# Early parts of chunks 14 to 23 in slots 7 to 10, a solver that fetches ahead, and seven block products from the fifth group on

## The chip, the cores and the metric

One core of a Trainium2 chip runs the kernel. The metric is the device time of one execution in microseconds. The engines are TensorE (PE in the rows, PEld for its weight loads), VectorE (DVE), ScalarE (ACT), GpSimd (POOL) and SyncE (SP), which here only issues transfers. Each engine works through its own instructions in the order in which the program gives them, and each queue of transfers is issued in that order too.

## What is computed

The first half is a recurrence over 768 tokens for 4 batches of 8 heads with 40 values each; the second half is a feed-forward layer on its output.

```python
for t in range(S):
    y[:, :, t] = einsum('bhd,bhde->bhe', r_t, state)
    Sa = einsum('bhde,bhe->bhd', state, a_t)
    state = state * w_t[:, :, None, :] - einsum('bhd,bhe->bhde', Sa, b_t)
    state = state + einsum('bhd,bhe->bhde', v_t, k_t)
x = y.transpose(0, 2, 1, 3).reshape(3072, 320)
h = maximum(x @ w_in, 0)            # w_in 320 x 2048
out = (h * h) @ w_out               # w_out 2048 x 320
```

Everything is float32.

## The kernel before

**Chunks.** The sequence is cut into chunks of 128 tokens of one batch: 24 chunks, numbered 0 to 23, four batches by six. For each chunk there are three kinds of work.

- The *early part* (`early`, L360) needs w, a and b only. It turns w (four transposes into one PSUM bank of the pool `ps_w`, which has four), runs the first scans over it on VectorE (L372, L373), then the second scans (L377 to L381), turns b and a, multiplies them by the decays (L387, L388), and makes the products N (matmuls into `ps_w`, copies on ScalarE). It yields after each of these, so a caller takes it in six steps. The decays are built in a ring of two tiles, `decay` (L186), stored to DRAM as `kept_e`, and come back later into `dec` (`kept_here`, also two). So chunks m and m + 2 write the same decay tile, and the second must wait until the first is stored. N goes to DRAM in pieces (`kept_q`, `kept_m`, `kept_n`, and from chunk 14 on `kept_d`). `prepare` (L907) wraps it: before the first step it starts the loads of w, b and a of the next chunk (`load_early`), on SP's queue.
- The *solve* inverts the triangular matrices of several chunks at once, a *unit*, on POOL: `take` fetches `kept_d` into `half_n`, `solving` runs 63 steps (two instructions each, L478 and L480; 31 steps for the units of chunks 0 to 13), and the result goes to `kept_t`. Units 0 to 7 hold chunks 0 to 13, unit 8 holds 14 to 17, unit 9 holds 18 to 21, unit 10 holds 22 and 23. `inverses` (L500) later fetches a chunk's share as T.
- The *chain* (`chain`, L632) uses T, N, the decays and the state of the batch, in eight steps, one of which needs the one before; its last instructions on VectorE are tokens (L697) and the new state (L701).

**The feed-forward layer** (`Ffn`, L724) works on groups of two chunks. `thirds` and `whole` make h, `square` squares it on VectorE, and `make_quarter` makes the output, four quarters for each chunk. From group SEVEN on `make_piece` takes the place of `make_quarter`'s matmuls: the output of two chunks is made from seven products of 128x160 blocks in place of eight, from sums and differences of blocks of h and of the weights. The sums of the weights (`sum_weights`, L875) are kept in the two `decay` tiles (P7, P6) and the four `in_ab` tiles (P4), one changes `w_out` in place, and one output tile lies in the first `in_w` tile. These tiles are free once no early part is left.

**The order** is written by hand; the engines get it as the program emits it. A list of words (L1013) orders chunks 0 to 6 and all of the early parts up to chunk 13, with their stores. Two words near its end matter below: `sE13@g` puts the store of chunk 13's decays on POOL's own queue, and `S6.99` has POOL finish unit 6; `S7.99` follows. After the list come 17 *slots* (L1125), i = 7 to 23. In slot i, `sorted_slot` (L1064) emits chunk i's chain, the preparations of chunk i + 1 (turning r and v, the products RV, decaying the state by f, L570, turning k, turning the decays, L582, scaling k and b, the products A), up to two early parts, and four quarters of the feed-forward layer. `ahead` (L1033) says which early parts a slot takes: 14 and 15 in slot 7, 16 and 17 in slot 8, and then one a slot, 18 to 23 in slots 9 to 14. The first of them is taken at fixed points of the slot from its start on, the second from the step of `turn_state` on, near its end. `step` emits a few things and then counts down stores that were put off (`tick`, `store`). At the slot's end `loads` starts the transfers of the chunk after the next: dec, k and b.

After a slot, every unit whose chunks all have their early parts is taken and solved whole: unit 8 after slot 8, unit 9 after slot 12, unit 10 after slot 14. One buffer `half_n` holds what a unit is solved from, so a unit's fetch starts when the one before is finished.

PSUM has eight banks: four in `ps_w`, two in `ps_c`, two in `ps_f`. A new tile of a pool takes a bank whose last reader is done, and the matmul that writes it waits for that reader.

## Time and profile before

| | |
|---|---|
| median of three runs | 945.2 us (944.94 to 946.49) |
| the profiled execution | 944.9 us, of it a span of 943.2 us |
| mean granted TensorE clock | 0.956 |
| transfers | 103.41 MB, of 253269 packets 234154 are under 512 B |

Times in rows are microseconds from the span's start. A row of a timeline has the start, the duration, the engine, the line, the operation, the tile written and the tiles read, and how many instructions are merged; in brackets stands how long the engine was idle before and what ended it. A row of a window has its bounds and length, then busy time and instructions of PE, PEld, DVE, ACT and POOL, the granted clock, the DMA share and GB/s. The DMA share counts packets in flight and can exceed 1 in short windows. A row of grouped instructions has the count, the busy time, the mean duration in ns and the idle time before. tokens (L697) of chunks 7 to 11 are written at 359.40, 396.29, 432.74, 466.72 and 500.69 us, so a slot takes some 34 to 37 us there.

### The profile page before, as it was taken

How to read it: one execution, taken by the hardware profiler on the slowest of the kernel's cores; microseconds unless marked ns; L12 is line 12 of the kernel's file. 1: busy time of each engine (PE TensorE's matmuls, PEld its weight loads, DVE VectorE, ACT ScalarE, POOL GpSimd, SP SyncE). 2: the span in 40 equal slices, each digit the busy share in tenths (PEclk: the TensorE clock that was granted, in tenths of full speed). 3: DMA queues.
4: the chain of work that ended last, by engine and by line, in shares of the span. 5: the costliest groups of instructions: out<-in, count | busy, mean ns of one | idle time of the engine just before them, and what ended most of it. 6: DMA issues, size and time to landing. Idle time of an engine off the chain costs nothing.

```text
span 943.2 us, 23218 instructions
## 1 busy us (share of the span) xinstructions
PE 883.6 (94%) x9404; PEld 738.8 (78%) x9404; DVE 518.8 (55%) x1209; ACT 283.0 (30%) x735; POOL 525.1 (56%) x935
## 2 busy tenths in 40 slices
PE   6678989889999999999999999999989999999997
PEld 5466657667787887888888888888978999988897
DVE  5827657888853454553755454675634645343243
ACT  3033334544523333333333332222212222222110
POOL 4557347065007786418999959999958986000000
PEclk9858988799899999999999999999998999999999
DMA  9769779766866578987665776604355445040000
GB/s 110 127 145 143 171 136 180 184 160 129 178 101 154 93 128 161 170 163 131 126 92 87 127 178 113 115 17 86 57 131 93 74 81 99 18 75 1 22 15 15
DMA packets 253269, 103.41 MB, mean 110 GB/s; under 512 B 234154, under 2 KB 240298, under 8 KB 252010
## 3 DMA queue, kind: packets, MB, share of 16 engines
q1 hardware_dynamic: 244709, 83.00, 49.7%
q0 software_dynamic: 3760, 17.10, 7.4%
q10 hardware_dynamic: 4693, 1.83, 0.9%
q8 instruction: 74, 1.21, 0.6%
q14 instruction: 33, 0.27, 0.1%
HBM read 69.00 MB, written 30.92 MB: 106 GB/s over the span
## 4 chain that ended last, share of the span: by engine, by line
PE 47%; POOL 25%; DVE 11%; DMA 8%; issue 4%; ACT 3%; SPq 2%; ACTq 0%; DVEq 0%; POOLq 0%
PE ps_f L87 21%; POOL half_t L480 13%; POOL half_p L478 12%; PE ps_w L87 11%; PE ps_c L87 8%; PE ps_w L331 3%; DMA half_n<-kept_d 2%; PE ps_f L264 2%; DMA in_r<-in_r_dram 1%; DMA T<-kept_t 1%; SPq L513 1%; DVE half_t L480 1%; DVE half_t L478 1%; DVE decay L381 1%; DMA dec<-kept_e 1%
## 5 line engine op out<-in xcount | busy, mean ns | idle before, releaser
L478 POOL TENSOR_TENSOR half_p<-half_n,half_t 128x462 f32<-128x462 f32 (+39 forms) x406 | 229.2, 565 | 75.7 <-DMA half_n<-kept_q 23.7
L480 POOL TENSOR_TENSOR half_t<-half_t,half_p 128x462 f32<-128x462 f32 (+39 forms) x406 | 245.7, 605 | 31.8
L87 PE MATMUL ps_f<-w_out,hid 128*128 128x320 f32 (+1 forms) x768 | 165.4, 368 | 0.0
L87 PE MATMUL ps_f<-tokens,w_in 128*128 128x256 f32 x672 | 157.0, 387 | 0.0
L87 PEld LDWEIGHTS ps_f<-w_out,hid 128*128 128x128 f32 x768 | 123.2, 190 | 26.0
L87 PEld LDWEIGHTS ps_f<-tokens,w_in 128*128 128x128 f32 x672 | 125.9, 192 | 19.1 <-issue 2.0
L769 DVE TENSOR_TENSOR hid<-hid 128x512 f32<-128x512 f32 x96 | 82.3, 899 | 10.3 <-ACT hid L762 9.9
L762 ACT ACTIVATE hid<-ps_f 128x512 f32<-128x512 f32 x84 | 49.8, 596 | 80.9 <-PE ps_f L87 80.8
L372 DVE TENSOR_TENSOR_SCAN decay<-ps_w,ones 128x64 f32<-128x64 f32 x88 | 23.9, 271 | 66.1 <-PE ps_w L331 66.0
L451 POOL DMA_DIRECT2D half_n<-kept_q x18 | 9.5, 534 | 88.7 <-DMA kept_m<-N 26.4
L697 DVE TENSOR_TENSOR tokens<-ps_c,dec 128x512 f32<-128x512 f32 x24 | 16.6, 691 | 72.9 <-PE ps_c L87 71.1
L347 DVE TENSOR_TENSOR RX<-ps_w,upper 128x512 f32<-128x512 f32 x48 | 30.8, 684 | 38.4 <-PE ps_w L87 38.2
L87 PEld LDWEIGHTS ps_c<-xr,T 64*64 64x64 f32 x768 | 29.7, 146 | 25.2 <-issue 18.4
L264 PE MATMUL ps_f<-ident 128*128 128x512 f32 (+3 forms) x108 | 49.4, 591 | 0.0
L87 PE MATMUL ps_f<-tokens,w_third 64*128 64x256 f32 x336 | 47.6, 394 | 0.1
L398 ACT COPY N<-ps_w 128x256 f32<-128x256 f32 x48 | 17.7, 369 | 94.9 <-PE ps_w L87 67.7
L548 DVE TENSOR_TENSOR kvT<-ps_w,dec 128x512 f32<-128x512 f32 x24 | 16.4, 684 | 52.5 <-PE ps_w L331 23.3
L87 PE MATMUL ps_c<-xr,T 64*64 64x40 f32 x768 | 35.7, 240 | 10.1 <-DMA T<-kept_t 5.4
L347 DVE TENSOR_TENSOR RV<-ps_w,upper 128x512 f32<-128x512 f32 x48 | 30.9, 685 | 21.2 <-PE ps_w L87 20.9
L658 ACT COPY minus_x<-ps_c 64x160 f32<-64x160 f32 x96 | 27.5, 287 | 36.5 <-PE ps_c L87 32.6
L331 PE MATMUL ps_w<-ident,in_ab 128*128 128x128 f32 x184 | 28.5, 301 | 10.1 <-DVE RV L347 8.1
L87 PE MATMUL ps_w<-rT,kvT 40*128 40x128 f32 x384 | 31.4, 308 | 5.4 <-ACT kvT L561 5.1
(167 smaller groups left out, 1548.9 us busy)
## 6 DMA issues: line engine op xcount, KB each, us to landing
dec<-kept_e SPq DMA_DIRECT2D x22, 633.8 KB
kept_e<-decay SPq DMA_DIRECT2D x19, 633.8 KB
in_w<-in_w_dram SPq DMA_DIRECT2D x24, 160.0 KB
in_b<-in_b_dram SPq DMA_DIRECT2D x24, 160.0 KB
in_ab<-in_a_dram SPq DMA_DIRECT2D x24, 160.0 KB
in_r<-in_r_dram SPq DMA_DIRECT2D x24, 160.0 KB
in_v<-in_v_dram SPq DMA_DIRECT2D x24, 160.0 KB
in_k<-in_k_dram SPq DMA_DIRECT2D x22, 160.0 KB
```

Source lines behind the costliest of these rows:

```text
L87: nc.tensor.matmul(o, l_, r_, start=start, stop=True, skip_group_check=True)
L264: nc.tensor.matmul(fill_bank[:, :n * 128], ident, ident.unsqueeze(1).to_broadcast([128, n, 128]), start=True, stop=True, skip_group_check= ...
L331: nc.tensor.transpose(p_[:, q * 128:(q + 1) * 128], pair(x_, q), ident)
L347: nc.vector.tensor_tensor(t_, p_, over4(upper), Alu.mult)
L372: nc.vector.tensor_tensor_scan(up[:, q, MID + 1:C + 1], wT[:, q, MID:], ones, 1.0, Alu.mult, Alu.mult)
L398: nc.scalar.copy(plain, p_[:, ::2].rearrange("s h (f t) -> s f h t", f=2))
L478: eng.tensor_tensor(p_, part[:, at:at + m_].unsqueeze(1).to_broadcast([128, n, m_]), t3[:, :n, s:s + 1].to_broadcast([128, n, m_]), Alu.mult)
L480: eng.tensor_tensor(t3[:, :n, s + 1:], t3[:, :n, s + 1:], p_, Alu.subtract)
L658: nc.scalar.copy(flipped(xn)[halves[half], flip, :, :, :D], by_pair(xs[halves[half ^ flip]]))
L697: nc.vector.tensor_tensor(t_, y_, g["up"][:, :, :C], Alu.mult)
L762: nc.scalar.activation(h_, p_.rearrange("p f t -> p (f t)"), Act.Relu)
L769: nc.vector.tensor_tensor(h_, h_, h_, Alu.mult)
```

## The change

- `ahead` puts the early parts of chunks 14, 15 and 16 into slot 7, of 17, 18 and 19 into slot 8, of 20 and 21 into slot 9, of 22 and 23 into slot 10. Slots 11 to 14 have none.
- A slot has 14 numbered places (`at_place`), most of them at the end of a step. The first early part of a slot takes its six steps at places 1 to 6, a middle one (made[1] of three) at 5 to 10, the last one at 9 to 14. Place 1 follows the turning of r and v, place 3 f and the decay of the state, place 4 the products RV and `thirds`, place 6 `whole`, place 8 precedes the turn of k, place 9 follows the turn of the decays, place 10 precedes the transposes of the chain's result, place 11 follows the scaling of k and b, place 12 the products A, place 13 `whole`, place 14 stands at the slot's end.
- Units are solved by `solve_more`: the first 32 rows' words of the next unit are fetched while the last 23 steps of the one before run, and unit 8 starts at place 9 of slot 8, unit 9 at the end of slot 9, unit 10 at the end of slot 10 (in POOL's order, each behind the unit before).
- SEVEN is 4 and not 6: groups 4 and 5 (chunks 8 to 11) take seven products too. The sums of the weights move from slots 15 and 16 to slots 11 and 12, the first of them to a point ahead of f, the second to a point behind f rather than behind the turn of k; the other two keep their points within a slot.
- In the last group the two last products get PSUM banks of their own, the additions of the two products before are done ahead of the last product, and chunk 23's output tile is stored one piece earlier.

```diff
+            last = g == len(order) // GB - 1
-            if at in (0, 3, 4):
-                self.bank = psum(ps_f)
+            fresh = at in ((0, 3, 4, 5, 6) if last else (0, 3, 4))
+            if fresh:
+                self.bank = psum(ps_w if at > 4 else ps_f)
...
+            if at == 4:
+                self.sixth = ps[0]
+            if at == (4 if last else 6):
+                plus(hi1, self.sixth, hi1)
+                plus(hi0, self.sixth, hi0)
+                less(lo1, hi1, lo1)
+            if at == 5:
+                self.fifth = ps[1]
+            if at == (5 if last else 6):
+                plus(hi1, self.fifth, hi1)
+                plus(hi0, self.fifth, hi0)
             if at == 6:
                 plus(hi0, ps[2], hi0)
-                plus(hi1, ps[0], hi1)
-                plus(hi0, ps[0], hi0)
-                less(lo1, hi1, lo1)
-                plus(hi0, ps[1], hi0)
-                plus(hi1, ps[1], hi1)
-                for n, o_ in enumerate(self.ends):
-                    bb, c = order[g * GB + n]
-                    row = bb * S + c * C
-                    store(out[row:row + C, :], o_, 2)
+            for n in {5: (1,), 6: (0,)}.get(at, ()) if last else (1, 0) if at == 6 else ():
+                bb, c = order[g * GB + n]
+                row = bb * S + c * C
+                store(out[row:row + C, :], self.ends[n], 2)
...
-    SEVEN = 6
+    SEVEN = 4
...
-    ahead = {7: (14, 15), 8: (16, 17)}
-    ahead.update({i: (i + 9,) for i in range(9, len(order) - 9)})
+    ahead = {7: (14, 15, 16), 8: (17, 18, 19), 9: (20, 21), 10: (22, 23)}
...
-    unit = len(solves)
+    under_way = [len(solves), None]
+
+    def solve_more():
+
+        u, now = under_way
+        while u < len(units) and all(m_ in done for m_ in range(len(order)) if unit_of[m_] == u):
+            flush()
+            take(u, own, slice(0, EARLIER))
+            if now is not None:
+                run(now)
+            take(u, own, slice(EARLIER, None))
+            now = solving(u, (40,))
+            next(now)
+            u += 1
+        if u == len(units) and now is not None:
+            run(now)
+            now = None
+        under_way[:] = u, now
...
-        one, two = (made + [iter(()), iter(())])[:2]
+        parts = [(gen, 1) for gen in made[:1]] + [(gen, 5) for gen in made[1:-1]] + [(gen, 9) for gen in made[1:][-1:]]
+        place = [0]
+
+        def at_place():
+            place[0] += 1
+            for gen, first in parts:
+                if first <= place[0] < first + 6:
+                    next(gen, None)
+            if i == 8 and place[0] == 9:
+                done.add(ahead[i][0])
+                solve_more()
...
-        step(of(turn_rv), on(one), on(one))
+        step(of(turn_rv), at_place)
         fetch_next(j + 1, "r")
-        step(second.make_quarter)
-        step(on(ch), of(decay_state))
-        if i == 2 * SEVEN + 3:
-            sum_weights(0)
-        if i == 2 * SEVEN + 4:
-            sum_weights(3)
-        step(of(make_rv), second.thirds)
-        step(on(ch), on(one))
+        sums(0)
+        step(second.make_quarter, at_place)
+        step(on(ch), of(decay_state), at_place)
+        sums(1, 3)
+        step(of(make_rv), second.thirds, at_place)
+        step(on(ch), at_place)
         if fine:
             join()
-        step(second.whole)
-        step(on(ch))
-        step(on(one), of(turn_k))
+        step(second.whole, at_place)
+        step(on(ch), at_place)
+        step(at_place, of(turn_k))
-        step(of(turn_down))
-        step(on(one), on(ch))
-        step(on(ch), of(scale_kb))
+        step(of(turn_down), at_place)
+        step(at_place, on(ch))
+        step(on(ch), of(scale_kb), at_place)
...
-        step(second.square, second.make_quarter, on(two), on(two))
-        if i in ahead and len(ahead[i]) > 1:
-            step(on(two), on(two))
-        step(second.make_quarter, on(two))
+        step(second.square, second.make_quarter, at_place)
+        step(second.make_quarter)
...
-        done.update(ahead.get(i, ()))
         sorted_slot(i, g, ch)
-        while unit < len(units) and all(m_ in done for m_ in range(len(order)) if unit_of[m_] == unit):
-            flush()
-            take(unit, own)
-            solve(unit)
-            unit += 1
+        done.update(ahead.get(i, ()))
+        solve_more()
```

More of the change, by code (lines that the diff above doesn't have):

```diff
@@ L797, in make_piece @@
         def make_piece(self, g, at):
-            names = "P1 P4 P2 P7 P6 P5 P3" if g == len(order) // GB - 1 else "P4 P1 P2 P7 P6 P5 P3"
+            last = g == len(order) // GB - 1
+            names = "P1 P4 P2 P7 P6 P5 P3" if last else "P4 P1 P2 P7 P6 P5 P3"
             if at == 7:
@@ L820, in make_piece @@
                 k, e, m_ = n // 4, n // 2 % 2, n % 2
-                mm(ps[part], x_[:, n], seven[name][k * QF + 2 * m_ + e], at in (0, 3, 4) and n == 0)
+                mm(ps[part], x_[:, n], seven[name][k * QF + 2 * m_ + e], fresh and n == 0)
             self.quarter += 1
@@ L1076, in sorted_slot, with sums @@
         of = lambda fn: (lambda: fn(j, n)) if more else (lambda: None)
+        def sums(*which_):
+            for n_ in which_:
+                if i == 2 * SEVEN + 3 + n_ // 3:
+                    sum_weights(n_)
         if more and "x" in n:
@@ L1084, in sorted_slot @@
             join()
-        step(of(turn_rv), on(one), on(one))
+        step(of(turn_rv), at_place)
         fetch_next(j + 1, "r")
-        step(second.make_quarter)
-        step(on(ch), of(decay_state))
-        if i == 2 * SEVEN + 3:
-            sum_weights(0)
-        if i == 2 * SEVEN + 4:
-            sum_weights(3)
-        step(of(make_rv), second.thirds)
-        step(on(ch), on(one))
+        sums(0)
[4 more added lines that the diff above has]
+        step(on(ch), at_place)
         if fine:
             join()
-        step(second.whole)
-        step(on(ch))
-        step(on(one), of(turn_k))
-        if i == 2 * SEVEN + 3:
-            sum_weights(1)
-        step(of(turn_down))
-        step(on(one), on(ch))
-        step(on(ch), of(scale_kb))
+        step(second.whole, at_place)
[4 more added lines that the diff above has]
+        step(on(ch), of(scale_kb), at_place)
         if fine:
             join()
-        step(on(ch), of(make_a), second.thirds, on(one))
+        step(on(ch), of(make_a), second.thirds, at_place)
         fetch_next(j + 1, "v")
-        step(of(turn_state), second.square, second.whole, on(two))
-        if i == 2 * SEVEN + 3:
-            sum_weights(2)
+        step(of(turn_state), second.square, second.whole, at_place)
+        sums(2)
         if not early_join and not fine:
@@ L1117, in sorted_slot @@
         loads(j + 1)
-        step(second.square, second.make_quarter, on(two), on(two))
-        if i in ahead and len(ahead[i]) > 1:
-            step(on(two), on(two))
-        step(second.make_quarter, on(two))
-        for gen in (one, two, joining):
+        step(second.square, second.make_quarter, at_place)
+        step(second.make_quarter)
+        for gen in made + [joining]:
             run(gen)
```

2 lines of the change are left out of this document (1 added, 1 removed).

## The prediction, on record before the changed kernel ran

> **What bounds the kernel now.** I read the busy shares first, then the windows by slot, the waits of TensorE, and the timeline of each engine and of the SP queue around slots 7 to 10, where the early parts go.
>
> ```profile
> PE 883.6 (94%) x9404; PEld 738.8 (78%) x9404; DVE 518.8 (55%) x1209; ACT 283.0 (30%) x735; POOL 525.1 (56%) x935
> 396.30:432.70 36.40, 35.96 (x444) 30.20 (x440) 20.23 (x60) 13.52 (x39) 8.22 (x17) 1.00 0.99 168
> PE ps_c L87 <- DMA T<-kept_t: 5.4, 1, 5.4
> ```
>
> TensorE is busy for 94% of the span, and from slot 7 on it hardly stops (35.96 of 36.40 us in the window about slot 8). So a microsecond that TensorE waits there is lost, and work that only changes its slot is free. After 330 us its one long wait is for T of chunk 18, the inverse that POOL solves as part of unit 9. The same window has a DMA share of 0.99 with two early parts in a slot; the change asks for three in slots 7 and 8.
>
> **What the change gains.** The wait for T, and what follows it:
>
> ```profile
> 479.64 0.66 PE L87 MATMUL ps_c<-xr,T 64*64 64x40 f32 x16
> ...
> 482.19 0.66 PE L87 MATMUL ps_c<-minus_x,N 64*64 64x40 f32 x16
> ...
> 708.54 1.08 PE L87 MATMUL ps_c<-xr,T 64*64 64x40 f32 x16 [5.36 <-DMA T<-kept_t]
> ...
> 713.27 0.66 PE L87 MATMUL ps_c<-minus_x,N 64*64 64x40 f32 x16
> ```
>
> ```profile
> 706.00:708.00 2.00, 0.00 (x0) 0.00 (x0) 0.00 (x0) 0.00 (x0) 0.15 (x1) 0.62 0.92 170
> 708.00:710.00 2.00, 1.46 (x20) 1.41 (x22) 0.00 (x0) 0.32 (x2) 1.61 (x6) 0.50 0.05 13
> ```
>
> ```profile
> 415.18 1.04 POOL L451 DMA_DIRECT2D half_n<-kept_d  x2 [25.14 <-DMA kept_d<-N]
> 693.76 0.60 POOL L487 DMA_DIRECT2D kept_t<-half_t  x1 [0.30 <-POOL half_t L480]
> ```
>
> The wait is 5.36 us. Behind it the clock is at half, and the stretch from the product with T to the one with N takes 713.27 - 708.54 = 4.73 us, against 482.19 - 479.64 = 2.55 us for the same work in slot 11. Together 5.36 + 2.18 = 7.5 us. POOL works from 415.18 to 693.76 on units 8 and 9. In the new order chunk 17 is ready by place 6 of slot 8, so unit 8 starts some 10 us earlier even if that slot is late, and the first words of unit 9 come in beneath unit 8's last steps. T of unit 9 then lands tens of us before its use if TensorE is late itself, and 10 to 20 us before it if not. I count the whole **-7.5**.
>
> The clock's price is told by the Trainium skill too (TensorE: Matmul & The Clock Gate, Part 1): an idle window of about 3.4 us halves the clock, and about 3.4 us of work restores it. By that an interruption would cost some 1.7 us behind it, not the 2.2 measured here. The trace decides.
>
> Two more groups take seven products:
>
> ```profile
> L87 PE MATMUL ps_f<-w_out,hid 128*128 128x320 f32 x32 | 9.0, 436 | 0.0
> ...
> L87 PE MATMUL ps_f<-w_out,hid 128*128 128x160 f32 x32 | 4.5, 299 | 0.0
> L87 PE MATMUL ps_f<-in_ab,hid 128*128 128x160 f32 x16 | 2.7, 312 | 0.1
> L87 PE MATMUL ps_f<-decay,hid 128*128 128x160 f32 x16 | 2.3, 299 | 0.0
> ...
> L87 PE MATMUL ps_f<-w_out,hid 128*128 128x160 f32 x32 | 4.5, 299 | 0.0
> L87 PE MATMUL ps_f<-decay,hid 128*128 128x160 f32 x16 | 2.4, 306 | 0.0
> ```
>
> The first row is one slot with the plain product (568.3 to 601.1 us), the next three and the last two are slots with block products (from 662.8 and 759.8). A group is two slots: 18.0 us plain, 9.5 + 6.9 = 16.4 us in blocks, so 1.6 us less; the busy sums count overlapping edges twice, more of them in blocks, so I take 2.0. Two groups: **-4.0** (3.2 to 5). Its additions on VectorE lie beside matmuls, in slots that lose an early part, and the weight sums move with it at the same cost.
>
> The tail of the last group:
>
> ```profile
> 938.44 0.33 DVE L825 TENSOR_TENSOR o<-ps_f,o 128x160 f32<-128x160 f32 x1 [6.19 <-PE ps_f L87]
> ...
> 939.61 0.32 DVE L825 TENSOR_TENSOR in_w<-ps_f,in_w 128x160 f32<-128x160 f32 x1
> ...
> 940.11 0.42 SPq L110 DMA_DIRECT2D out_dram<-in_w  x1
> ```
>
> One of the six additions stays behind the last matmul, and one store, issued at about 938.8 in place of 940.11: **-1.3**. The small wait for bT when a second early part is run in one go at a slot's end (below, 0.44) goes too: **-0.4**. Gains: 7.5 + 4.0 + 1.3 + 0.4 = 13.2 us.
>
> **What it costs.** An early part moved from slots 11 to 14 into slots 7 to 10 carries these matmuls, and nine transfers on SP's queue:
>
> ```profile
> 476.95 0.60 PE L331 MATMUL ps_w<-ident,in_w 128*128 128x128 f32 x4
> ...
> 487.02 1.09 PE L331 MATMUL ps_w<-ident,in_ab 128*128 128x128 f32 x8
> ...
> 493.64 1.06 PE L87 MATMUL ps_w<-decay,bT 40*128 40x128 f32 x16
> ```
>
> That is 0.60 + 1.09 + 1.06 = 2.75, with overlaps some 2.4 us, paid now or later. The price is in the order. Slot 7, now:
>
> ```profile
> 334.37 0.60 PE L331 MATMUL ps_w<-ident,in_w 128*128 128x128 f32 x4
> ...
> 339.61 0.66 PE L87 MATMUL ps_c<-minus_x,N 64*64 64x40 f32 x16
> ...
> 344.44 1.09 PE L331 MATMUL ps_w<-ident,in_ab 128*128 128x128 f32 x8
> ...
> 346.61 0.66 PE L582 MATMUL ps_w<-ident,dec 128*128 128x128 f32 x4 [0.63 <-DVE decay L381]
> ...
> 367.27 1.16 PE L87 MATMUL ps_w<-decay,bT 40*128 40x128 f32 x16 [0.44 <-DVE decay L388]
> ```
>
> ```profile
> 341.88 0.17 DVE L570 TENSOR_TENSOR f<-end,dec 128x4 f32<-128x4 f32 x1 [5.32 <-DMA dec<-kept_e]
> ...
> 344.32 0.17 DVE L377 RECIPROCAL decay<-decay 128x4 f32<-128x4 f32 x1
> ...
> 361.99 0.29 DVE L372 TENSOR_TENSOR_SCAN decay<-ps_w,ones 128x64 f32<-128x64 f32 x1
> ...
> 363.28 0.27 DVE L373 TENSOR_TENSOR_SCAN decay<-ps_w,ones 128x64 f32<-128x64 f32 x1
> ```
>
> *First, the second decay tile.* The ring `decay` has two tiles, so chunk 15 writes the tile of chunk 13, and must wait until chunk 13's decays have been stored. Chunk 15 now writes at 361.99. The store goes out on POOL, behind the steps of a solve:
>
> ```profile
> 353.82 0.56 POOL L390 DMA_DIRECT2D kept_e<-decay  x1
> ```
>
> ```profile
> kept_e<-decay POOLq DMA_DIRECT2D x1, 633.8 KB, 5.8
> ```
>
> So the tile is free at 353.82 + 5.8 = 359.6. In the new order chunk 15 is made[1]: turned at place 5, scanned at place 6, which VectorE reaches near 348. VectorE works in order, so the first scans stand until 359.6; behind them wait the other scans, kvT, the scaling of k and b, the masks RX and A. First scans 363.28 + 0.27 - 361.99 = 1.5 us, second scans 346.61 - 344.32 = 2.3 us: done at 363.4. TensorE goes on with chunk 14's product, chunk 15's turns and k, until it runs out of PSUM: of the four ps_w banks one holds chunk 15's turned w until the second scans have read it, and the other three wait for VectorE's products behind them. So the turn of the decays (L582) cannot begin before 363.4; now it begins at 346.61. That is 16.8 us later, of which 2.4 are work done earlier: 14.4, and about 1.4 more for the clock, since part of the slow stretch waits for bT anyway. **+15.8** (12 if the store lands sooner or the clock holds, 18).
>
> An earlier wait in slot 7 lies inside this one: chunk 14's b and a are now turned at place 4, at about 340 and not 344.44, and the fourth bank is that of its w, whose second scans now stand behind f (341.88, held up by the decays of chunk 8) rather than behind RV. That is 5 us of waiting, but the point at 363.4 does not move with it.
>
> *Second, slot 8's loads.* Chunk 18 is fetched when chunk 17 starts (place 1) and turned at place 5, four places later; now a second part starts only near the slot's end. SP's queue in slots 7 and 8:
>
> ```profile
> 360.06 1.20 SPq L146 DMA_DIRECT2D in_w<-in_w_dram  x1
> ...
> 362.91 6.41 SPq L710 DMA_DIRECT2D tokens<-tokens  x8
> 369.43 0.47 SPq L1049 DMA_DIRECT2D dec<-kept_e  x1
> ...
> 378.11 4.63 SPq L110 DMA_DIRECT2D kept_d<-N  x4
> ...
> 383.40 0.58 SPq L146 DMA_DIRECT2D in_w<-in_w_dram  x1
> ```
>
> The fetch asked for at slot 8's start goes out at 383.40, because the decays, k, b, blocks, N and the stores stand before it. One fetch of three leaves the place ahead of the tokens (362.91 - 360.06 = 2.9 us) and one store of decays (0.5), so about 380 on this slot's clock, and in_w lands perhaps 4 us later (between 2 and the 5.8 of the larger store): 384. Place 5 comes at about 378. TensorE waits 0 to 6 us, with the clock 0 to 8.5; I take **+5**, below the middle of what the queue gives, because slot 7's stop lets the queue drain.
>
> *Third, the last part of a slot* is scanned at places 10 and 11, between kvT and RX; its four microseconds of scans stand before the masks and hold a bank that the products A need. By the same scans (1.5 + 2.3 us) against some 3 us of TensorE work: about 1.2 us in each of slots 8, 9 and 10, with one wait for bT: **+3** (0 to 5).
>
> *Fourth, slot 10*, whose f waits for its decays as well:
>
> ```profile
> 447.35 0.17 DVE L570 TENSOR_TENSOR f<-end,dec 128x4 f32<-128x4 f32 x1 [2.18 <-DMA dec<-kept_e]
> ```
>
> As in slot 7 the turns of place 4 now stand behind it: **+1** (0 to 2.5).
>
> Sum: 15.8 + 5 + 3 + 1 - 13.2 = +11.6 on the profiled execution's 944.9 us, which lies 0.3 below the median of 945.2: 956.5; I say **956.5 us**. Its own range, with all bounds of one sign, is 946 to 967.
>
> **The rivals.** *A, the tile is free in time.* If the store of chunk 13 landed by about 348, or the scans of chunk 15 reached VectorE only at 360, the 15.8 and its sequel vanish, as the slot then runs as the two-part slots do now: 944.9 - 13.2 = 931.7, at worst 935 with the smaller waits. From a landing near 350 on, it is no longer faster: 13.2 of gains less 9 of other costs leaves 4. For it: POOL would run quicker while VectorE stands. Against: the store is behind POOL's steps, and nothing before slot 7 is changed. Chance 0.10.
>
> *B, the stop in slot 7 alone.* The queue drains during it, so that slots 8 to 10 cost nothing: 944.9 - 13.2 + 15.8 = 947.5, or 943 to 945 where the block products give the upper end. For it: SP idles while TensorE stands. Against: the fetch's place in the queue. Chance 0.12.
>
> *C, the queue does not recover.* With three stores and three fetches a slot against a DMA share of 0.99 every transfer of slots 8 to 10 comes late, the decays first, and each slot has a stop like slot 7's first, 5 + 2 us: 956.5 + 14 = 970. Against: with one part a slot, that share fell back by itself. Chance 0.05.
>
> **How the numbers follow.** Forecast 0.73, A 0.10, B 0.12, C 0.05. 943 to 968 holds nearly all of the forecast and most of B, 0.8 together. A measurement of this kernel tells 0.2%, 1.9 us, from no change. Faster: A, and a little of B and the forecast's low end, 0.14. Same (943.3 to 947.1): half of B, 0.07. Slower: the rest, 0.79.
>
> **What would show it.** Right: in slot 7 VectorE's first scans of the second early part waiting some 11 us for kept_e, TensorE's turn of dec waiting for decay L381, slot 7 about 18 us longer, the granted clock at half behind it; a wait of TensorE for in_w in slot 8; no wait for T near 700; fewer than six additions behind the last matmul. Wrong: slots 7 and 8 of some 39 us each, or a second early part whose scans find their tile free.

## The result, and the profile after

The changed kernel takes 975.25 us (median of 5 runs, 972.57 to 979.39), the kernel before 944.94 us beside it (942.95 to 946.49). The ratio is **1.0322 [1.0289, 1.0355]**: 30 us slower, where 11.6 were forecast and 968 was the upper end of the range. The profiled execution took 973.1 us with a span of 971.4.

The windows of the changed kernel from one chunk's tokens to the next, for chunks 7, 8, 11 and 12 (columns as in the table of windows shown for the kernel before: length, busy time of PE, PEld, DVE, ACT and POOL, granted clock, DMA share, GB/s):

```profile
322.30:381.20 58.90, 46.22 (x450) 38.03 (x450) 26.97 (x82) 16.87 (x49) 44.34 (x114) 0.83 0.65 128
381.20:431.40 50.20, 43.78 (x481) 35.69 (x477) 25.06 (x81) 16.03 (x47) 13.44 (x34) 0.90 0.77 158
...
511.80:546.80 35.00, 33.46 (x411) 26.99 (x405) 20.11 (x26) 11.61 (x31) 32.49 (x33) 1.00 0.52 101
546.80:581.50 34.70, 32.15 (x394) 26.08 (x390) 12.58 (x21) 9.41 (x23) 24.50 (x46) 1.00 0.46 103
```

The first two of them in the kernel before:

```profile
323.30:359.40 36.10, 35.47 (x416) 29.66 (x416) 16.62 (x43) 14.59 (x41) 26.74 (x69) 1.00 0.64 123
359.40:396.30 36.90, 36.46 (x451) 30.76 (x447) 20.50 (x61) 13.65 (x39) 23.42 (x63) 1.00 0.82 153
```

I call such a stretch a row, by the chunk whose tokens end it (VectorE's L697). The first row was 36.13 us before, the second 36.89. Both now lose time twice: TensorE stands for 12.7 and 6.4 us of them, and their mean granted clock is 0.83 and 0.90 where it was 1.00. All rows, from the same instruction in both traces, beside what the prediction's terms add up to (its 2.4 us of moved work per part counted in rows 7 to 10 and taken off from row 11 on):

| rows | before | after | difference | forecast |
|---|---|---|---|---|
| start to tokens of chunk 6 | 323.27 | 322.27 | -1.0 | 0 |
| 7 | 36.13 | 58.98 | +22.9 | +17.8 |
| 8 | 36.89 | 50.14 | +13.3 | +8.4 |
| 9 | 36.45 | 39.47 | +3.0 | +3.4 |
| 10 | 33.98 | 40.92 | +6.9 | +4.4 |
| 11 and 12 | 67.94 | 69.74 | +1.8 | -4.8 |
| 13 to 17 | 158.88 | 149.00 | -9.9 | -8.8 |
| 18 | 35.82 | 28.49 | -7.3 | -7.5 |
| 19 to 23 | 142.93 | 142.93 | 0.0 | 0 |
| tokens of chunk 23 to the end | 70.9 | 69.5 | -1.4 | -1.3 |

The gains came as forecast, 18.6 us against 17.6 in the last rows with the moved work. The costs were 18.7 us higher than forecast: 5.1 in row 7, 4.9 in row 8, 2.5 in row 10 and 6.6 in rows 11 and 12, less 0.4 in row 9.

What TensorE waited for after 322 us (sum, times, longest):

```profile
PE ps_w L331 <- issue: 9.5, 2, 7.7
PE ps_c L671 <- ACT minus_x L658: 5.8, 5, 2.5
PE ps_w L331 <- DVE decay L381: 4.9, 1, 4.9
PE ps_w L331 <- DMA in_w<-in_w_dram: 3.9, 1, 3.9
PE ps_w L87 <- ACT xnT L673: 1.6, 1, 1.6
```

The wait for T is gone. In its place are these five kinds of wait in rows 7 to 12 (of the rest, none sums to over 0.8 us). Row 7, from the timelines of TensorE and VectorE, and windows of 4 us:

```profile
344.14 1.09 PE L331 MATMUL ps_w<-ident,in_ab 128*128 128x128 f32 x4 [4.88 <-DVE decay L381]
...
358.28 0.29 DVE L372 TENSOR_TENSOR_SCAN decay<-ps_w,ones 128x64 f32<-128x64 f32 x1 [11.56 <-DMA kept_e<-decay]
...
362.21 1.09 PE L331 MATMUL ps_w<-ident,in_ab 128*128 128x128 f32 x4 [7.72 <-issue]
...
363.94 1.06 PE L582 MATMUL ps_w<-ident,dec 128*128 128x128 f32 x4
```

```profile
344.00:348.00 4.00, 3.86 (x27) 3.29 (x28) 2.72 (x5) 1.38 (x4) 3.29 (x10) 0.50 1.31 178
...
356.00:360.00 4.00, 0.00 (x0) 0.00 (x0) 1.69 (x10) 0.25 (x1) 0.07 (x1) 0.62 0.98 261
360.00:364.00 4.00, 1.79 (x9) 1.82 (x10) 2.11 (x10) 0.00 (x0) 3.14 (x12) 0.50 0.42 71
364.00:368.00 4.00, 3.92 (x25) 3.11 (x23) 3.73 (x12) 0.00 (x0) 3.29 (x10) 0.50 0.49 100
368.00:372.00 4.00, 4.00 (x56) 3.63 (x54) 2.65 (x12) 3.09 (x11) 3.37 (x9) 0.67 0.47 129
```

This is the stop that the prediction described: VectorE stands 11.56 us for the store of chunk 13, and the turn of dec starts at 363.94, where the prediction has 363.4 as its earliest time. In part that nearness is chance, as the row itself starts 1.0 us sooner here (322.27 against 323.27): from the row's start it is 41.67 us, and 40.1 by the prediction. Behind the stop the clock stays at half to about 370.

Row 8, from the timelines of SP's queue, TensorE and ScalarE:

```profile
399.86 0.59 SPq L146 DMA_DIRECT2D in_w<-in_w_dram  x1
...
403.64 1.09 PE L331 MATMUL ps_w<-ident,in_w 128*128 128x128 f32 x4 [3.95 <-DMA in_w<-in_w_dram]
...
417.16 0.37 ACT L398 COPY N<-ps_w 128x256 f32<-128x256 f32 x1 [3.13 <-DMA kept_n<-N]
...
419.98 1.16 PE L87 MATMUL ps_w<-rT,xnT 40*128 40x128 f32 x16 [1.57 <-ACT xnT L673]
```

The late w is there. Not foreseen is the second half: the one tile N of an early part is still being stored when the next part wants it, ScalarE waits with its copies, and the copy to xnT, which the chain needs, stands behind them in ScalarE's order.

The gains, from the timelines of TensorE and VectorE: chunk 18's products without a wait, and one addition behind the last matmul.

```profile
740.09 0.66 PE L87 MATMUL ps_c<-xr,T 64*64 64x40 f32 x16
...
742.91 0.66 PE L87 MATMUL ps_c<-minus_x,N 64*64 64x40 f32 x16
...
968.09 0.33 DVE L827 TENSOR_TENSOR o<-ps_w,o 128x160 f32<-128x160 f32 x1 [1.62 <-PE ps_w L87]
```

### The profile page after: what moved, and what is told of

Read it like the earlier page. It is cut to its first block, busy times and chain, and to the rows that moved or that the text cites. A ratio compares the mean times of both kernels' runs of the same rounds, so it can differ in the third digit from the quotient of the medians.

```text
span 971.4 us, 23479 instructions
## 1 busy us (share of the span) xinstructions
PE 893.6 (92%) x9500; PEld 750.5 (77%) x9500; DVE 531.9 (55%) x1233; ACT 283.1 (29%) x735; POOL 531.7 (55%) x943
## 4 chain that ended last, share of the span: by engine, by line
PE 75%; DVE 8%; DMA 6%; ACT 5%; issue 4%; SPq 2%; POOL 0%; ACTq 0%; DVEq 0%; POOLq 0%
PE ps_f L87 37%; PE ps_w L87 15%; PE ps_c L87 12%; PE ps_w L331 5%; PE ps_f L264 2%; PE ps_c L671 1%; DMA blocks<-kept_t 1%; ACT N L401 1%; PE ps_c L598 1%; DMA hid<-in_moe_w_in_dram 1%; SPq L420 1%; DVE half_t L478 1%; DVE half_t L480 1%; PE ps_w L582 1%; DMA dec<-kept_e 1%
## 5 line engine op out<-in xcount | busy, mean ns | idle before, releaser
L480 POOL TENSOR_TENSOR half_t<-half_t,half_p 128x462 f32<-128x462 f32 (+39 forms) x406 | 250.5, 617 | 31.8
L87 PE MATMUL ps_f<-tokens,w_in 128*128 128x256 f32 x672 | 160.5, 394 | 0.0
L87 PEld LDWEIGHTS ps_f<-tokens,w_in 128*128 128x128 f32 x672 | 128.8, 197 | 20.1 <-issue 2.2
L87 PE MATMUL ps_f<-w_out,hid 128*128 128x160 f32 (+1 forms) x736 | 143.4, 348 | 0.0
L87 PEld LDWEIGHTS ps_f<-w_out,hid 128*128 128x128 f32 x736 | 112.7, 190 | 17.3
L769 DVE TENSOR_TENSOR hid<-hid 128x512 f32<-128x512 f32 x96 | 78.8, 862 | 9.9 <-ACT hid L762 9.4
L331 PE MATMUL ps_w<-ident,in_ab 128*128 128x128 f32 x184 | 30.6, 310 | 25.9 <-issue 10.6
L697 DVE TENSOR_TENSOR tokens<-ps_c,dec 128x512 f32<-128x512 f32 x24 | 16.6, 691 | 64.6 <-PE ps_c L87 62.8
L331 PEld LDWEIGHTS ps_w<-ident,in_ab 128*128 128x128 f32 x184 | 23.2, 158 | 32.5 <-issue 17.6
L87 PE MATMUL ps_f<-decay,hid 128*128 128x160 f32 x256 | 38.0, 302 | 0.4 <-DVE hid L828 0.4
```

The costliest lines, as they stand in the source:

```text
L87: nc.tensor.matmul(o, l_, r_, start=start, stop=True, skip_group_check=True)
L331: nc.tensor.transpose(p_[:, q * 128:(q + 1) * 128], pair(x_, q), ident)
L480: eng.tensor_tensor(t3[:, :n, s + 1:], t3[:, :n, s + 1:], p_, Alu.subtract)
L697: nc.vector.tensor_tensor(t_, y_, g["up"][:, :, :C], Alu.mult)
L769: nc.vector.tensor_tensor(h_, h_, h_, Alu.mult)
```

## The experiments

Ratios are to the kernel before, run beside each. The start to chunk 6's tokens took between 316.8 and 323.3 us in the profiles though hardly anything differs there, so I compare rows first and totals second.

**The store of chunk 13 alone.**

```diff
-... D8 sE13@g K7 S7.99 lk8
+... D8 sE13 K7 S7.99 lk8
```

> One edit to the changed kernel (973.1 us profiled, 975.25 median): the store of chunk 13's decays goes out on SP's queue and not on POOL's, behind the steps of a solve. Theory of the prediction (chunk 15's scans wait for that store): VectorE's wait of 11.56 us for kept_e at L372 and TensorE's second stop in slot 7 (7.72 us at the turn of b and a) go; slot 7 (r-turn to tokens, 48.75 us) falls to about 35, since the first stop (4.88 us at place 4, and its clock) stays; total 958 to 966. Rival (three early parts are simply too much for slot 7, whatever the tile): another wait takes its place, slot 7 stays over 44 us and the total over 970.

Measured: 967.76 us, ratio 1.0260 [1.0233, 1.0288]. Row 7 is 53.29 us and not 58.98: 5.7 less, where about 14 was expected. Timelines of VectorE and TensorE in this kernel, and its windows:

```profile
347.41 0.29 DVE L372 TENSOR_TENSOR_SCAN decay<-ps_w,ones 128x64 f32<-128x64 f32 x1 [0.60 <-PE ps_w L331]
...
362.91 2.08 PE L87 MATMUL ps_w<-rT,xnT 40*128 40x128 f32 x16 [2.87 <-ACT xnT L673]
```

```profile
360.00:364.00 4.00, 1.14 (x14) 1.10 (x12) 1.12 (x5) 3.40 (x11) 3.26 (x10) 0.80 1.22 216
364.00:368.00 4.00, 4.00 (x34) 3.50 (x32) 2.57 (x5) 0.00 (x0) 3.33 (x9) 0.50 0.76 172
368.00:372.00 4.00, 4.00 (x23) 3.47 (x22) 2.91 (x5) 0.58 (x1) 3.53 (x7) 0.84 0.15 34
```

The store was the cause of the second stop: the scans now wait 0.60 us. But a later wait, for xnT, had lain hidden behind it, and the clock is at half behind that one too. So the theory was right about this wait and wrong about its price. In the expectation's own measure, from the turn of r to the tokens, the slot is 43.1 us (375.68 - 332.62): well over the theory's 35 and just under the rival's 44. The rival's other wait did appear, but the total lies between the two ranges.

**The scans ahead of f.**

```diff
-        step(on(ch), of(decay_state), at_place)
+        step(on(ch), at_place, of(decay_state))
```

> One edit to the changed kernel: at place 3 the second scans of a slot's first early part are put ahead of f (VectorE's first use of the next chunk's decays), not behind it. TensorE's order is unchanged. In slots 7 and 10 TensorE's turn of b and a waited for these scans, which stood behind f and so behind dec's transfer. Theory of the prediction (in slot 7 the first stop lies inside the second, whose end is set by the store of chunk 13): the stop of 4.88 us goes, but TensorE then meets the second one earlier and the turn of dec (L582) stays near 363.5; slot 7 (58.98 us from tokens to tokens) falls by under 2.5 us, slot 10 (40.92) by 2 to 4; total 970 to 973. Rival (the two stops add up): slot 7 falls by 5 to 8 us, total 965 to 968.

Measured: 968.87 us, ratio 1.0247 [1.0191, 1.0303]. Row 7 is 60.47 us (58.98), row 10 38.90 (40.92). The timelines of VectorE and TensorE:

```profile
354.03 0.29 DVE L372 TENSOR_TENSOR_SCAN decay<-ps_w,ones 128x64 f32<-128x64 f32 x1 [14.13 <-DMA kept_e<-decay]
...
357.97 1.09 PE L331 MATMUL ps_w<-ident,in_ab 128*128 128x128 f32 x4 [10.62 <-issue]
...
359.70 1.06 PE L582 MATMUL ps_w<-ident,dec 128*128 128x128 f32 x4
```

The turn of dec starts 42.32 us behind the last tokens (359.70 - 317.38), against 363.94 - 322.27 = 41.67. The first stop is gone, the second is 2.90 us longer (10.62 against 7.72), and the turn of dec starts no sooner: the first lay inside the second, as the prediction said. In row 10, where no second stop follows, the same edit is worth 2.0 us. The total fell more than these rows, since the opening was 4.9 us shorter in this profile than in that of the change.

**Both together.**

> Both edits together: the store of chunk 13's decays on SP's queue (slot 7: 53.29 us, where a stop of 4.85 us at the turn of b and a and one of 2.87 us for xnT are left) and the second scans ahead of f. Theory (the stop behind f is what is left of slot 7's loss, and the wait for xnT follows from the time lost before): slot 7 falls to 43 to 47 us, slot 10 by 2 to 4, total 955 to 960 against 967.8 of the store alone. Rival (ScalarE's copies of N for three parts are in the way of xnT by themselves): the wait for xnT stays or grows to 4 us and more, slot 7 over 48 us, total over 962.

Measured: 963.48 us, ratio 1.0193 [1.0131, 1.0255]. Row 7 is 52.11 us, 1.2 less than with the store alone; the theory fell. TensorE's timeline:

```profile
343.69 1.09 PE L331 MATMUL ps_w<-ident,in_w 128*128 128x128 f32 x4 [4.66 <-DMA in_w<-in_w_dram]
...
361.73 1.16 PE L87 MATMUL ps_w<-rT,xnT 40*128 40x128 f32 x16 [2.77 <-ACT xnT L673]
```

With the turn of b and a out of the way, TensorE reaches chunk 15's w at place 5 some 5 us before it has landed.

**Chunk 15's w from the opening as well.**

```diff
-... e13.5 c6 wh0 sN12 ... lk8
+... e13.5 LW15 c6 wh0 sN12 ... lk8 LA15
```

> The changed kernel with three edits for slot 7: the store of chunk 13's decays on SP's queue, the second scans ahead of f, and w of chunk 15 fetched in the opening (with these first two alone the slot is 52.11 us, and TensorE waits 4.66 us for this w, then 2.77 us for xnT). Theory (slot 7 has a row of waits one behind another, of which only the last-ending ones count: f, w of chunk 15, chunk 13's store, and the store of N ahead of xnT): the wait for in_w goes, the one for xnT stays, since N's one tile is still being stored: slot 7 falls to 45 to 48 us, total 955 to 960. Rival (each remedy only uncovers a next wait of the same length): slot 7 stays over 50 us, total 961 to 965.

Measured: 959.43 us, ratio 1.0172 [1.0118, 1.0225]. Row 7 is 48.48 us; the waits left there are 2.04 us (RV behind f), 0.54 and 2.74 (xnT). The total lies where the theory has it, the row 0.5 us above its 45 to 48; the wait behind f is one more than it named.

**The three-part slots moved on by one**, with the store of chunk 13 on SP's queue here too.

```diff
+    ahead = {7: (14, 15), 8: (16, 17, 18), 9: (19, 20, 21), 10: (22, 23)}
...
+            if i == 8 and place[0] == 12:
+                done.update(ahead[i][:2])
```

> The changed kernel with the store of chunk 13 on SP's queue, and the three-part slots moved one slot on: slot 7 makes two early parts, slots 8 and 9 three each, slot 10 two. Theory (three parts in a slot cost more than their work wherever they stand, since SP's queue and the one N tile serve two parts in time and not three): slot 7 falls to 38 to 42 us, slots 8 and 9 are 46 to 51 us each (36.9 and 36.5 in the kernel before, where a part is worth 2.4), total 955 to 963. Rival (slot 7 is the special one, behind the opening's transfers): slots 8 and 9 are 41 to 44 us, total 944 to 951.

Measured: 965.32 us, ratio 1.0216 [1.0160, 1.0271]. Rows 7, 8 and 9 are 45.37, 51.76 and 44.64 us. Row 7 has the same two parts as in the kernel before and is 9.2 us longer. TensorE's timeline shows a part of why:

```profile
343.16 1.08 PE L331 MATMUL ps_w<-ident,in_ab 128*128 128x128 f32 x4 [4.53 <-DVE decay L381]
```

So a part of row 7's loss, 9.2 us here, does not come from the third part. The wait shown, 4.53 us, comes from the new places, which put the turn of b and a behind f; the rest was not split further. Row 9 with three parts falls below the theory's 46; neither side was right about it.

**Row 8's fetch.**

```diff
+        if i in ahead and max(ahead[i]) + 2 < len(order):
+            load_early(max(ahead[i]) + 2)
         loads(j + 1)
```

> One edit to the changed kernel: w, b and a of chunks 18, 21 and 23 are asked for at the end of the slot ahead (before that slot's decays, k and b), not when the part before them starts. TensorE's order is unchanged. Theory (in slot 8 TensorE's wait of 3.95 us for in_w and the clock behind it are the price of the late fetch): that wait goes, slot 8 (50.14 us) falls by 5 to 7, total 967 to 971. Rival (the queue is full, a transfer put ahead only delays the decays, blocks and N behind it): in_w's wait goes but f waits longer for dec, slot 8 falls by under 2, total 973 to 977.

Measured: 973.56 us, ratio 1.0321 [1.0283, 1.0360]. Row 8 is 50.52 us (50.14). Timelines of VectorE and TensorE:

```profile
398.77 0.17 DVE L570 TENSOR_TENSOR f<-end,dec 128x4 f32<-128x4 f32 x1 [4.10 <-DMA dec<-kept_e]
...
401.98 1.08 PE L331 MATMUL ps_w<-ident,in_ab 128*128 128x128 f32 x4 [3.62 <-issue]
```

The wait for in_w is gone and the decays are late in its place; TensorE stops for 3.62 us behind f, as I read it through the bank that the scans behind f hold. The rival holds. The same edit fetches chunk 23 earlier too, and row 10 rises from 40.92 to 44.39 us, with a stop of 3.66 us at the same line.

**Row 8 with both of its waits mended**, that is, this fetch on top of the three edits for row 7:

> The three edits for slot 7 (store of chunk 13 on SP's queue, second scans ahead of f, w of chunk 15 in the opening: 959.4 us, slot 8 50.92 us) and the earlier fetch of chunks 18, 21 and 23. Theory (slot 8's price is in_w's late fetch and, once that is mended, the turn of b and a that waits behind f; with the scans ahead of f both are gone): the wait of 4.71 us for in_w and the clock behind it go and nothing takes their place, slot 8 falls to 42 to 46 us; POOL's handover at about 545 us then falls into the middle of slot 12 again; total 945 to 953. Rival (the queue's transfers only change places, so another one is late): a wait of 3 us or more for f, RV or kvT stands in slot 8, which stays over 48 us; total 957 to 962.

Measured: 962.92 us, ratio 1.0168 [1.0121, 1.0215]. Row 8 is 50.84 us. Timelines of VectorE, ScalarE and TensorE:

```profile
404.33 0.29 DVE L372 TENSOR_TENSOR_SCAN decay<-ps_w,ones 128x64 f32<-128x64 f32 x1 [4.12 <-DMA kept_e<-decay]
...
406.28 0.37 ACT L398 COPY N<-ps_w 128x256 f32<-128x256 f32 x1 [7.39 <-DMA kept_n<-N]
...
406.77 1.06 PE L87 MATMUL ps_w<-spares 32*32 32x32 f32 x32 [3.82 <-issue]
```

Of the wait for in_w 0.76 us is left, the one behind f is gone, and two stores are late in their place: of a decay tile (there are two) and of N (there is one). The rival holds again. Row 7, which the three edits had brought to 48.48 us, is 53.99 us here: in it ScalarE waits 8.26 us for N's store and TensorE 6.66 us for xnT. The earlier fetch is not the reason, as it goes out at 379.28, behind this row. What differs is POOL's store of the T of unit 6: here at 347.71, just ahead of N's store (348.31), there at 353.19, just behind it (352.91). That this costs the 5.5 us was not tested.

**Fewer bytes.** In the change, and in the kernel just shown:

```diff
-            store(kept_e[i], dec[:USED], 2)
+            rows_ = USED // 2 if 14 <= i < 20 else USED
+            store(kept_e[i][:rows_], dec[:rows_], 2)
...
```

The loads of these decays are cut to the same rows.

> The changed kernel with half of a transfer left out: of the decays of chunks 14 to 19 only rows 0 to 51 of 104 are stored, and loaded again in slots 13 to 18 (what is computed from chunk 14 on is not the reference's). Each of the six stores has 317 KB and not 634, so slot 8 moves some 7.0 MB and not 7.93; every instruction and its order stay. Theory (slot 8 is as long as the transfers of three parts take: 7.9 MB at the 168 GB/s that the fullest two-part slot of the kernel before ran at are 47 us, and each wait taken away uncovered another transfer): slot 8 falls from 50.1 us by 4 to 7, slot 7's second stop is unchanged (chunk 13's store is whole): total 966 to 971. Rival (latency and order of the single transfers, not their bytes, set slot 8): it falls by under 2 us, total 973 to 976.

> The same half stores of the decays of chunks 14 to 19 (the rest of the output as above) in the kernel that has the mended fetches, scans and store (slot 7 54.0, slot 8 50.8 us; there VectorE waited 4.12 us for kept_e and ScalarE 7.39 us for kept_n in slot 8, and TensorE 6.66 us for xnT in slot 7). Theory (bytes): these waits shrink with the stores, slots 7 and 8 fall by 4 to 8 us each, total 947 to 955 against 962.9. Rival (latency and order): slots 7 and 8 fall by under 2 us each, total 958 to 963.

Measured: 972.75 us, ratio 1.0314 [1.0263, 1.0366], row 8 50.45 us. Its window and TensorE's wait in it:

```profile
377.50:428.00 50.50, 43.67 (x480) 35.59 (x476) 25.16 (x81) 16.03 (x47) 15.06 (x38) 0.90 0.79 142
```

```profile
399.97 1.09 PE L331 MATMUL ps_w<-ident,in_w 128*128 128x128 f32 x4 [4.01 <-DMA in_w<-in_w_dram]
```

That is 50.5 us at 142 GB/s, 7.2 MB for 7.9 (50.2 at 158), and a wait for in_w as long as before. The other kernel took 961.72 us, ratio 1.0187 [1.0144, 1.0229], rows 7 and 8 52.83 and 47.36 us (53.99 and 50.84). So in the change itself the bytes of these stores do not set row 8: the theory fell. Where the fetches are mended and the stores wait last, half of the decays' bytes takes 1.2 us off row 7, as the rival has it, and 3.5 off row 8, between the two. What is left is the order and the latency of single transfers, on two decay tiles and one N tile; that is by exclusion, as no run changes these alone. A second N tile wasn't tried.

**Seven products.**

```diff
-    SEVEN = 4
+    SEVEN = 6
```

> One edit to the changed kernel: seven block products from the seventh group on, as before, not from the fifth. Theory of the prediction (two groups gain 4.0 us, 3.2 to 5): total 978 to 980.5. Rival (slots 12 to 15 are bound by something else there, so that the shorter products bring nothing): 974 to 976.5.

Measured: 974.15 us, ratio 1.0334 [1.0290, 1.0379]. The total does not tell: the four executions spread from 970.99 to 979.70 us, and their median lies where the rival has it. The profile is of the longest, in which row 12 alone took 41.20 us (34.73), behind the collision of the next paragraph. The rows that hold the products speak for the theory: row 14 30.31 us against 28.49, row 16 30.18 against 28.49, rows 13, 15 and 17 alike within 0.1. Together 3.5 us for two groups, in one profile of each kernel.

**The words of the next unit, fetched later or in one go.** Rows 11 and 12 had been expected 4.8 us shorter and were 1.8 longer. In the change, POOL hands over from unit 8 to unit 9 at 554 us, among the transfers of slot 12. One kernel fetches nothing ahead:

```diff
-            take(u, own, slice(0, EARLIER))
             if now is not None:
                 run(now)
-            take(u, own, slice(EARLIER, None))
+            take(u, own)
```

> One edit to the changed kernel: the words of the next unit are all fetched when the unit before has been solved (as in the kernel before), not in its last steps. Theory (the fetch of the words collides with the small transfers at the start of slots 11 and 12: f waits 7.20 and 10.34 us for dec, the copies behind T's blocks come late): with the fetch away from there those waits shrink to under 4 us, slots 11 and 12 are 2 to 4 us shorter each, total 967 to 971; T for chunk 18 is still in time, since TensorE is 28 us later than before. Rival 1 (the waits there come from the order of SP's queue, whatever POOL fetches): no change, 973 to 977. Rival 2 (T late again): a stop near 735, total about 982.

The other delays POOL:

```diff
-        eng.memset(ts, 0.0)
+        for _ in range(10 if u == 8 else 1): eng.memset(ts, 0.0)
```

> One edit to the changed kernel: unit 8's cleared tile is cleared ten times on POOL and not once, about 10 us more work there (it computes the same). So the fetch of unit 9's first words (510 us) and the store of T of unit 8 with the fetch of the rest (554 us) come 10 us later, behind the transfers with which slots 11 and 12 begin and not among them. Theory (these 0.5 to 1.8 MB collide with the decays, N and blocks of the slot's start; f waited 7.20 and 10.34 us): f's waits in slots 11 and 12 fall under 3 us, the two slots together (69.74 us) by 3 to 6, T for chunk 18 still in time, total 969 to 972. Rival (SP's queue is behind by itself after the three-part slots): the waits stay, total 974 to 977.

Measured: without the fetch ahead 977.85 us, ratio 1.0377 [1.0342, 1.0412]; row 11 33.14 us (35.01), row 12 44.10 (34.73). All words now come at 552 us, and row 12 is worse, as POOL's and TensorE's timelines show (minus_x is a copy by ScalarE that the chain needs):

```profile
552.52 1.03 POOL L451 DMA_DIRECT2D half_n<-kept_d  x2
...
569.81 1.21 PE L671 MATMUL ps_c<-ident,minus_x 128*128 128x128 f32 x4 [7.91 <-ACT minus_x L658]
```

So the theory's forecast fell: it had not seen that the fetch would go to row 12's start, where f still waits 10.29 us. With POOL late 965.26 us, ratio 1.0196 [1.0139, 1.0252]; rows 11 and 12 are 33.43 and 31.39 us, 4.9 less together. In the view of transfers of the change (size of each, us from issue to landing) between 500 and 580 us, these are what POOL's handover moves:

```profile
kept_t<-half_t POOLq DMA_DIRECT2D x1, 1024.0 KB, 8.3
half_n<-kept_d POOLq DMA_DIRECT2D x2, 256.0 KB, 9.6
```

ScalarE's copies out of blocks (a fetched share of T) in row 12, in the change and then with POOL late, the latter behind VectorE's f:

```profile
568.06 0.91 ACT L522 ACTIVATE T<-blocks,which 128x256 f32<-128x256 f32 x2 [4.88 <-DMA blocks<-kept_t]
```

```profile
555.11 0.48 DVE L570 TENSOR_TENSOR f<-end,dec 128x4 f32<-128x4 f32 x1 [9.68 <-DMA dec<-kept_e]
...
557.81 0.91 ACT L522 ACTIVATE T<-blocks,which 128x256 f32<-128x256 f32 x2
```

Beside POOL's store of T and fetch of words, ScalarE waits 4.88 us for blocks, and the copy to minus_x behind it comes late; without them it does not wait. With POOL late f still waited 9.68 us for dec, at no price; the landing of blocks was what mattered. Row 12 differs much from profile to profile: in the kernels of this section in which POOL hands over 5 to 12 us behind its start it takes 32.07 to 44.10 us. The kernel before had its handover at 549.91 us, 15.2 us behind chunk 12's tokens, in the middle of row 13. It is TensorE's own delay, 46 us by the start of row 12 (546.79 against 500.69), that moved a row's start under it.

**The fetch ahead alone in the kernel before.**

> The kernel before with one part of the change: the next unit's first words are fetched in a unit's last steps, and the early parts and the seven products stay as they were. Theory (T of chunk 18 comes in time, 5.36 us and the clock behind it): the stop in front of chunk 18's products goes, slot 18 falls from 35.8 to about 28.5 us, the fetch of unit 9's words at about 508 us costs under 2 us in slot 11; ratio to the kernel before 0.992 to 0.994. Rival (T is no earlier, since POOL's solve and not the fetch decides, or the fetch disturbs as much as it gains): 0.998 to 1.003.

Measured: 964.77 us, ratio **1.0190** [1.0110, 1.0270]; neither theory had it. Row 14 takes 47.50 us (32.83 in the kernel before). Timelines of POOL, TensorE and VectorE:

```profile
536.21 1.08 POOL L451 DMA_DIRECT2D half_n<-kept_d  x2 [33.58 <-DMA kept_d<-N]
...
586.57 1.08 PE L87 MATMUL ps_c<-xr,T 64*64 64x40 f32 x16 [3.61 <-DMA T<-kept_t]
...
599.00 0.17 DVE L570 TENSOR_TENSOR f<-end,dec 128x4 f32<-128x4 f32 x1 [16.60 <-DMA dec<-kept_e]
```

At step 40 of unit 8 the words of chunk 21 do not exist yet, with one part a slot. POOL stands for 33.58 us in the middle of unit 8, and T of chunk 14 is late; T of chunk 18 is late as well (row 18 takes 37.13 us). So the fetch at step 40 needs the early parts moved; the parts of the change lean on one another.

**The gains without the third part.** Two versions of the kernel before, both with the change's `solve_more` and its banks and additions in the last group. Beside these they have:

```diff
+    SEVEN = 5
...
+    ahead = {7: (14, 15), 8: (16, 17), 9: (18, 19), 10: (20, 21), 11: (22,), 12: (23,)}
...
+            now = solving(u, (46,))
```

> The kernel before with the placement of its early parts kept and never more than two in a slot (slots 7 to 10 two, 11 and 12 one), seven products from the sixth group on (SEVEN = 5), the tail's banks and additions of the change, and unit 9's first words fetched in unit 8's last steps, six steps later than in the change (at about 523 us, behind slot 11's first transfers). Theory (the gains of the change are real and only the third part costs): T for chunk 18 in time 7.3, tail 1.4, one group of seven products 1.8: ratio to the kernel before 0.987 to 0.991. Rival (four slots with two parts in a row are too many for SP's queue as well): slots 9 and 10 over 39 us each, ratio 0.994 to 1.000.

```diff
+            now = solving(u, (53,))
```

> The kernel before with two parts of the change that need no early part moved: the tail's banks and additions, and unit 9's first words fetched in unit 8's last steps, but at step 53 (about 541 us), when the words of chunk 21 have been stored (at step 40 POOL waited 33.58 us for them, and chunk 14's T came late). Theory (POOL's handover shrinks by 5 us, T of chunk 18 comes in time, the tail gives 1.4): slot 18 falls from 35.8 to 28.5 to 31 us, ratio 0.991 to 0.995. Rival (POOL still waits for chunk 21's stores or for the store of T before it may clear the tile, so T is no earlier): only the tail, 0.998 to 1.000.

Measured: with two parts a slot 942.50 us, ratio 0.9974 [0.9942, 1.0007]: no difference that can be told. Row 18 is 28.49 us, as wanted, but rows 9 to 12 are 39.20, 39.29, 37.63 and 39.77 us. The rival's figures came for rows 9 and 10, of which about 2.4 us each is the moved part's own work; the fetch at 519.57 us, 7.5 us behind chunk 11's tokens, met row 12's transfers again (TensorE waits 2.06 us for minus_x at 536.64). With the fetch at step 53 and the early parts left alone **933.10 us, ratio 0.9879 [0.9845, 0.9912]**: 1.2% faster than the kernel before. Its timelines of POOL and TensorE:

```profile
533.42 1.08 POOL L451 DMA_DIRECT2D half_n<-kept_d  x2
...
547.15 0.60 POOL L487 DMA_DIRECT2D kept_t<-half_t  x1 [0.30 <-POOL half_t L480]
...
554.93 0.29 POOL L478 TENSOR_TENSOR half_p<-half_n,half_t 128x63 f32<-128x63 f32 x1
...
687.09 0.60 POOL L487 DMA_DIRECT2D kept_t<-half_t  x1 [0.30 <-POOL half_t L480]
```

The handover, from the store of T to the next step, takes 554.93 - 547.15 = 7.8 us (12.4 before); T of unit 9 goes out at 687.09 and not at 693.76, row 18 is 28.49 us, and the tail 69.5 us. From chunk 6's tokens on that is 7.4 us; the rest of the difference of the medians lies in the opening, which this trace does not explain.

## Why the prediction was right or wrong

- **T's wait: the number right, the reason not.** -7.5 forecast, row 18 shows -7.3. The reason given, that unit 8 starts some 10 us earlier, was wrong: its words were fetched at 417.21 us (415.18 before), as POOL's timeline has it:

```profile
417.21 2.05 POOL L451 DMA_DIRECT2D half_n<-kept_d  x4 [27.75 <-DMA kept_n<-N]
```

  T of unit 9 left POOL at 697.80 us, 4 us later than before, and was in time because TensorE wanted it 37 us later (740.09 against 708.54 - 5.36 = 703.18). The prediction names this case ("if TensorE is late itself"), but then the fetch ahead does not earn the gain: without it row 18 is 28.49 us too. That the fetch can earn it where TensorE is not late is shown by the kernel with the fetch at step 53.
- **Seven products: right by the rows.** -4.0 (3.2 to 5) forecast, 3.5 measured; the totals neither confirm nor exclude it.
- **Tail: right.** -1.3 forecast, -1.4 measured, one addition behind the last matmul.
- **"First, the second decay tile": mechanism right, price wrong.** Store and wait came as written, and the first stop did lie inside the second. The turn of dec came 1.5 us later by the row's start, as from the first scan to it went 5.7 us (363.94 - 358.28) and not 3.8. The term that was mis-sized is "about 1.4 more for the clock": from the turn of dec to the tokens it took 381.25 - 363.94 = 17.3 us and not 359.40 - 346.61 = 12.8, so 4.5 more. Of these 0.9 are the turns of the third part's b and a, which now lie there; the other 3.6 or so are the clock's, at half to about 370. The wait for the store was also not the row's price by itself: without it the row falls by 5.7 us only, because f, in_w and N's store wait right behind. With store, f and in_w mended, row 7 is 48.48 us (53.99 and 52.83 in the two later kernels that have these edits) and still 12.4 over the kernel before.
- **"Second, slot 8's loads": the wait right, the price too low.** TensorE waited 3.95 us for in_w, within 0 to 6. But +5 took this wait for the whole row's cost, and the row lost 10.9 us net of 2.4 for the moved part. The step left out that a third part also needs the N tile and a decay tile back from their stores; row 8 stays between 48.7 and 51.8 us in all twelve kernels with three parts there, whichever wait is taken away, and falls to 47.36 only with mended fetches and half of the decays' stores left out.
- **"Third" and "Fourth": too low together.** ("Third" names about 1.2 us in each of three slots, which is 3.6 and not the 3 that it takes.) Row 9 came as forecast; row 10 lost 4.5 us net and not 2. Of these 2.0 are the turns behind f, by the run with the scans ahead of f; that mechanism was forecast at 1.
- **Missing altogether: rows 11 and 12**, 6.6 us against the forecast. The prediction costed POOL's new fetch as a gain only. That POOL's store of T and fetch of words, 1.0 and 0.5 MB, would meet a row's first transfers once TensorE is 46 us late was not considered; the delayed POOL shows it at 4.9 us. Of the rest 1.1 is a matter of the table: the last product of slot 10's second part falls behind chunk 10's tokens, and so into row 11.
- **Rivals.** A, the tile free in time, did not occur, and would not have given 931.7: with the store out of the way the kernel still takes 967.8. B, the later slots for nothing, is excluded by row 8. C was nearest in size (970), and its mechanism, transfers that come late in every three-part slot, is the one that rows 8 and 10 show, though not with a stop of 7 us in each.
- **The range.** With all bounds of one sign the prediction's own terms begin at 943 us (12 of cost less 14.2 of gains) and not at 946. The measured time lies beyond the other end, so this does not bear on the miss.

The step that failed is thus the cost of the third part. The 9 us for the waits of slots 8 to 10 were 16.0 (rows 8 to 10, the moved work taken off), the 1.4 for the clock in slot 7 some 3.6, and POOL's transfers in rows 11 and 12 were put at nothing and cost 4.9. The common error: each wait was priced alone, with the clock it costs, as if behind it the slot ran as before. The runs show rows of waits on the same queue and tiles, each hiding the next.

The Trainium skill (TensorE: Matmul & The Clock Gate, Part 1) has the clock fall after an idle window of about 3.4 us. The run with the store on SP shows half clock from 364 to 368 us behind a stop of 2.87 us, so here a shorter stop cost it too, and the measurement decides; by that rule the xnT waits would have been cheap.

## What to carry to other kernels

Before work is moved into a slot, list everything that it takes back from a transfer (tiles still being stored, words still being fetched) and how many copies there are; the slot's price is the chain of those waits, and removing the longest only shows the next. When one engine is made late, look at what the others do by their own clock: a harmless transfer of POOL became a collision because TensorE's slot slid under it. A gain that depends on a resource's timing may be had without the costly move: here a fetch at step 53 and the tail's banks gave all of T's wait and of the tail.

## What was not expected of the hardware

- Two fetches of 64 KB on SP's queue landed late beside one fetch of 0.5 MB and one store of 1 MB by POOL: ScalarE waited 4.88 us for them, and not at all with POOL late. The time for which they hold SP's queue does not tell it: it is 9.10 us in the change and 4.46 with POOL late, but 4.47 with the scans ahead of f, where POOL's transfers come at the same place and ScalarE waited 5.10 us.
- Half the bytes of the decays' stores left a wait for another transfer as it was in the changed kernel: TensorE's wait for in_w was 4.01 us with 7.2 MB in the row and 3.95 with 7.9.
- A stop of 2.87 us cost the clock as one of 4.88 did: 0.50 in the window that follows (364 to 368 us there; 344 to 348 in the change).
